# Attention into a gated FFN on one core: head 0's bias rows made in place, pads and V's ones set later on VectorE, a key row and a cast moved in front of V's loads

## The chip, the core and the metric

The kernel runs on one core of a Trainium2 chip. Its engines are TensorE (PE in the profile; its weight loads are PEld), VectorE (DVE), ScalarE (ACT), GpSimd (POOL) and SyncE (SP), each with its own instruction queue, and 16 DMA engines that all queues share. The metric is the device time of one execution in microseconds (us); the profile's times are those of one profiled execution.

## The reference

Eight batches of eight heads, 576 positions, head dimension 64. Selective attention: a causal softmax whose scores carry a bias from the running sum of the positive part of s. Its output, seen as 4608 tokens of 512, goes through a gated FFN of width 1536.

```python
def _attn_ref(q, k, v, s):
    scores = (1.0 / np.sqrt(D)) * np.matmul(q, k.transpose(0, 1, 3, 2))
    cum = np.cumsum(np.maximum(s, 0.0), axis=-1)
    bias = -(cum[:, :, :, None] - cum[:, :, None, :])
    scores = np.where(causal, -1000000000.0, scores + np.minimum(bias, 0.0))
    attn = softmax(scores)
    return np.matmul(attn, v)

def _moe_ref(x, w_gate, w_val, w_out):
    g = x @ w_gate
    return (g * sigmoid(g) * (x @ w_val)) @ w_out
```

All inputs and the output are float32.

## The kernel before

**Tiling.** Heads come in "head batches" of four (`hb`, 16 of them); head batch 0 is heads 0 to 3, head batch 1 heads 4 to 7. For each, k and q are loaded as float32 (`load_one`), cast to bf16 (`cast_half`, `cast_one`), transposed, and copied into `KQ[hb % 2][r]`. There are two such tiles per head batch, r = 0 for its first two heads and r = 1 for the others; in the text r is the row half. In the tile, 64 partitions hold the transposed k and q of those two heads, one beside the other (`e`), and the other 64 hold bias rows, of which four are used and the rest are zero. Thus one matmul of 128 partitions gives scores and bias together: the cumulated s is split into a high and a low bf16 part (`HL`), which stand in the query's or the key's rows against rows of constants near 1 and -1 (`ONES2`, `NEGS2`, each a 32-bit word holding two bf16). `aug` brings four bias rows of a head from `HL` into the tile by a DMA on SP's queue. `pads` zeroes 64 columns behind the keys, since the last key chunk of a head is 128 wide and reads 64 columns further.

**Scores and values.** `score_piece(bh, ci)` makes one of four pieces of a head's scores in a bank of PSUM (pieces 0 and 3 begin with a matmul of a mask, `lower`), and ScalarE's exponential (L369) takes it to `pt`. `av_piece` multiplies `pt` with `VT`, V in bf16 with a column of ones for the sum; `av_out` divides (L412, L413). `x_pe` transposes the attention output for the FFN. `init_vt` writes VT's ones and the zeros below its fifth chunk.

**The first stage.** The head batches 0 and 1 do not go through DRAM: TensorE transposes them against the identity (`pe_transpose_half`, L301; `pe_transpose`, L287) and `pe_out` copies from PSUM to `KQ` (L316 on VectorE, L314 on ScalarE). Of the eight banks, `take` gives the one that was given back longest ago, in program order. One bank (`spare`) serves `keep_warm`, matmuls of the identity whose result nobody reads; four hold the transposes of a head batch until the second row half is copied out.

**Order.** The program is under a manual schedule: each engine executes its instructions in the order written, and waits only for what an instruction needs. The order of the first stage is written out by hand. On VectorE: constants, the chain from s to `HL` (L226 to L232), copies of q for head batch 0, casts and copies of head batch 1, the cast of V's last chunk. On POOL: the mask, zeroes, the loads of head batch 1, `init_vt` and pads, a cast of q, V's loads (five DMAs), a weight load, casts of V. SP has s, the four loads of head batch 0, and then the `aug` DMAs, which follow from L232.

From head 8 on, a generator (`attn_items`) is pumped between the FFN's matmuls (L630, L687, L736).

## Time and profile before

| what | value |
|---|---|
| median of 5 runs | 375.87 us (375.82 to 377.81) |
| profiled execution | 375.86 us |
| its span | 374.1 us |
| mean granted TensorE clock | 1.000 |
| TensorE busy | 364.8 us (98%) |
| VectorE, ScalarE, POOL busy | 290.1, 240.7, 212.9 us |
| first exponential of scores | 11.36 us |
| first matmul of values | 19.54 us |

The span runs from the first to the last instruction; the execution's time has 1.8 us around it. Times in the profile count from the start of the span. A row of the timeline gives start, length, engine, line, operation, what it writes and reads with the shape, and how many; in brackets stand the idle time of the engine ahead of it and what ended it. A row of the waits gives the engine and line that waited, what for, the sum of the waits in us, their number, and the longest. Lines are those of the kernel before.

### The profile page before, as it was taken

What the parts mean: (1) busy time and instruction counts of PE and PEld (TensorE: products, weight loads), DVE (VectorE), ACT (ScalarE), POOL (GpSimd) and SP (SyncE); (2) the same over time, 40 slices, a digit from 0 to 9 for tenths busy, and PEclk for the clock granted to TensorE, in tenths of its full rate; (3) what the DMA queues carried; (4) which work ended last, traced back from release to release, by engine and by line L of the source; (5) the groups of instructions that cost most, each with busy time, mean ns of one, the idle gap of its engine ahead of it and who ended that gap; (6) DMA issues with size and microseconds to landing.
All of it is one profiled execution on the core that took longest, in us unless ns stands there. A gap on an engine that the chain in (4) does not pass through costs nothing.

```text
span 374.1 us, 8800 instructions
## 1 busy us (share of the span) xinstructions
PE 364.8 (98%) x3300; PEld 231.6 (62%) x3300; DVE 290.1 (78%) x578; ACT 240.7 (64%) x471; POOL 212.9 (57%) x325
## 2 busy tenths in 40 slices
PE   7899999999999999999999999999999999999995
PEld 6575556555555556855685559655865585476464
DVE  8968776468985999589967997699858867975984
ACT  8877776688876878588757875686566523323321
POOL 8982655856465647494649564955675516315320
PEclk9999999999999999999999999999999999999999
DMA  7799999799599997895879665995132103002003
GB/s 240 192 269 260 214 270 249 233 341 209 175 185 280 252 264 199 166 281 203 227 165 268 181 172 161 271 186 122 40 119 62 35 19 128 2 0 95 19 0 114
DMA packets 97147, 64.23 MB, mean 172 GB/s; under 512 B 77233, under 2 KB 82737, under 8 KB 97105
## 3 DMA queue, kind: packets, MB, share of 16 engines
q1 hardware_dynamic: 84976, 41.46, 46.8%
q0 software_dynamic: 12128, 22.21, 22.2%
q8 instruction: 26, 0.43, 0.5%
q14 instruction: 17, 0.13, 0.1%
HBM read 37.90 MB, written 19.86 MB: 154 GB/s over the span
## 4 chain that ended last, share of the span: by engine, by line
PE 90%; POOL 3%; ACT 2%; DVE 2%; issue 1%; DMA 1%; DVEq 0%; POOLq 0%; ACTq 0%
PE bank L630 47%; PE bank L736 17%; PE bank L359 11%; PE bank L396 8%; PE bank L687 6%; ACT pt L369 2%; DVE kq L316 1%; DMA kq<-HL 1%; PE bank L446 1%; DVE pp L653 1%; PE bank L287 1%; POOL vt L168 1%; DVE ht L664 1%; PE bank L353 1%; ACT kq L314 0%
## 5 line engine op out<-in xcount | busy, mean ns | idle before, releaser
L369 ACT ACTIVATE pt<-bank 128x512 bf16<-128x512 f32 (+1 forms) x256 | 120.3, 509 | 30.2 <-PE bank L359 17.0
L630 PE MATMUL bank<-XT,wg 128*128 128x512 bf16 x432 | 111.4, 379 | 0.5 <-DVE pp L653 0.3
L630 PE MATMUL bank<-XT,wv 128*128 128x512 bf16 x432 | 110.9, 379 | 0.1
L651 ACT ACTIVATE th<-bank 128x512 bf16<-128x512 f32 x108 | 64.7, 599 | 55.7 <-PE bank L630 52.2
L653 DVE SCALAR_TENSOR_TENSOR pp<-th,bank 128x512 bf16<-128x512 bf16 x108 | 73.6, 682 | 18.8 <-ACT th L651 18.3
L664 DVE SCALAR_TENSOR_TENSOR ht<-pp,bank 128x512 bf16<-128x512 bf16 x108 | 74.1, 686 | 10.6 <-PE bank L630 0.4
L359 PE MATMUL bank<-kq 128*128 128x128 bf16 (+4 forms) x576 | 75.8, 240 | 1.0 <-DMA kq<-HL 0.5
L673 POOL TENSOR_TENSOR ht<-ht 128x512 bf16<-128x512 bf16 x35 | 40.5, 1156 | 52.1 <-DVE su L671 52.0
L359 PEld LDWEIGHTS <-kq 128*128 128x128 bf16 x576 | 45.8, 98 | 31.4 <-issue 1.9
L630 PEld LDWEIGHTS <-wv 128*128 128x128 bf16 x432 | 38.4, 98 | 36.4 <-issue 0.6
L630 PEld LDWEIGHTS <-wg 128*128 128x128 bf16 x432 | 38.3, 98 | 34.2 <-issue 0.7
L374 POOL TENSOR_SCALAR_AFFINE_SELECT pt<-pt 128x512 bf16<-128x512 bf16 x56 | 36.9, 659 | 28.4 <-ACT pt L369 22.7
L396 PEld LDWEIGHTS <-pt 128*128 128x128 bf16 x960 | 41.7, 98 | 17.3
L396 PE MATMUL bank<-vt,pt 128*128 128x65 bf16 x960 | 46.9, 194 | 0.3 <-POOL vt L168 0.3
L430 POOL DMA_DIRECT2D xs<-ot x24 | 21.7, 906 | 29.9 <-DVE ot L413 27.6
L736 PEld LDWEIGHTS <-ht 128*128 128x128 bf16 x336 | 31.2, 98 | 4.3
L413 DVE TENSOR_TENSOR ot<-bank,rc 128x320 bf16<-128x320 f32 x64 | 31.4, 491 | 2.2
L183 POOL DMA_DIRECT2D kq<-HL x48 | 29.0, 606 | 0.0
L687 PE MATMUL bank<-wo,ht 128*128 128x512 bf16 x96 | 25.8, 379 | 0.0
L736 PEld LDWEIGHTS <-su 128*128 128x128 bf16 x252 | 23.6, 98 | 3.3
L801 POOL TENSOR_TENSOR ysb<-ysb 128x512 f32<-128x512 f32 x12 | 15.2, 1270 | 15.3 <-DVE ysb L795 15.3
L379 POOL TENSOR_SCALAR_AFFINE_SELECT pt<-pt 128x64 bf16<-128x64 bf16 x56 | 14.9, 267 | 15.6 <-ACT pt L369 15.5
(93 smaller groups left out, 388.0 us busy)
## 6 DMA issues: line engine op xcount, KB each, us to landing
out_dram<-ysb POOLq DMA_DIRECT2D x32, 256.0 KB, 4.5
rawv<-in_v_dram SPq DMA_DIRECT2D x28, 256.0 KB
rawk<-in_k_dram SPq DMA_DIRECT2D x12, 576.0 KB
rawq<-in_q_dram SPq DMA_DIRECT2D x12, 576.0 KB
xs<-ot POOLq DMA_DIRECT2D x24, 160.0 KB, 3.8
ks<-ck SPq DMA_DIRECT2D x11, 288.0 KB
qs<-cq SPq DMA_DIRECT2D x11, 288.0 KB
rawk<-in_k_dram POOLq DMA_DIRECT2D x3, 576.0 KB, 6.7
```

Of the source, the lines that this page charges most:

```text
L359: nc.tensor.matmul(sc[:, o : o + w], T[:, 1, e * S + 128 * tj : e * S + 128 * (tj + 1)], T[:, 0, e * S + lo : e * S + hi], start=not maske ...
L369: nc.scalar.activation(pt[:, c0 : c0 + n], sc, AF.Exp, scale=0.125)
L374: nc.gpsimd.affine_select(pt[:, 1088:1600], pt[:, 1088:1600], pattern=[[0, 4], [1, 128]], compare_op=ALU.is_ge, fill=zreg, base=0, channel ...
L396: nc.tensor.matmul(av[:, bi * (D + 1) : (bi + 1) * (D + 1)], pt[:, c0 : c0 + 128], VT[b % 2][:, tj, h, :], start=(tj == 0), stop=(tj == bi),)
L413: nc.vector.tensor_mul(ot[:, :, e * D : (e + 1) * D], av3[:, :, 0:D], rc[:, :, None].to_broadcast([128, NCH, D]),)
L630: nc.tensor.matmul(view(bs, TT), w[:, c, f0 : f0 + 128], xt[:, c, :], start=(c == 0), stop=(c == 3),)
L651: nc.scalar.activation(th, pg, AF.Tanh, scale=0.5)
L653: nc.vector.scalar_tensor_tensor(pp, in0=th, scalar=1.0, in1=pg, op0=ALU.add, op1=ALU.mult)
L664: nc.vector.scalar_tensor_tensor(hp[:, 2 * k2 : 2 * k2 + 2, :].rearrange("p a n -> p (a n)"), in0=pp, scalar=0.5, in1=pv, op0=ALU.mult, op ...
L673: (nc.vector if ft == NFT - 1 else nc.gpsimd).tensor_sub(hp[:, 1:3, :], hp[:, 1:4:2, :], hp[:, 0:3:2, :])
L687: nc.tensor.matmul(view(pys[ts_], DM), hps[ft // 2][:, 2 * (ft % 2) + half, c0 : c0 + 128], WO[j][:, ft % WKO, :], start=(ft == 0), stop=( ...
L736: nc.tensor.matmul(ps, lhs(p), rhs(p), start=(first and p == 0), stop=(last and p == NP - 1), skip_group_check=True,)
```

## The change

- `s_sb`, `c8` and `HL` get two more partitions (64 and 65). A second load, on ScalarE's queue, brings head 0's s into both.
- A column `less` is -1 everywhere but 0 in partition 64. The low part is now `less * high + c8`; so partition 64 holds the whole sum, rounded to bf16 (its high part) and partition 65 the low part, next to each other. The same instruction does both.
- Two engine copies put these two rows into head 0's key half (POOL, partitions 64 and 65) and query half (VectorE, partitions 96 and 97) of `KQ[0][0]`; the constants against them are two memsets on POOL. `aug` leaves head 0 out. Partitions 96 and 97 are zeroed on POOL before head batch 2 uses the tile.
- ScalarE zeroes one tile instead of two, POOL the other.
- On POOL the copy of the key row and the cast of q stand in front of V's loads with `init_vt(0)` and `pads(1)` gone from there; the memset of `aug_rows(1, 1)` goes behind V's loads. `pads(1)` and `init_vt(0)` move to VectorE, among and behind the copies of head batch 1.
- The second k copy of row half 1 goes from ScalarE to VectorE. The first three score pieces of head 0 stand between the k and q transposes of row half 1, and the fourth behind them; each of the two groups of ten keep-warm matmuls shrinks to four.
- The transposes of head batch 1 stand inside head 2 (behind its second and its fourth piece) instead of behind heads 0 and 1. The values of heads 0 and 1 go behind the scores of head 6.

```diff
--- before.py
+++ after.py
@@ -78,6 +78,7 @@
     )
 
     NPE = 5
+    LR = 66
     XB = 2
     KS = {i: dram.tile([NR * S, 128], BF16, name=f"ks{i}") for i in range(NPE, NHB)}
     XS = {
@@ -95,15 +96,16 @@
     VT = [const.tile([128, NCH, H, D + 1], BF16, name=f"vt{i}") for i in range(2)]
     ident = const.tile([128, 128], BF16)
     one_s = const.tile([128, 1], FP32)
-    HL = const.tile([BH, 4, 2, S], BF16)
+    HL = const.tile([LR, 4, 2, S], BF16)
     XR = 3 * TT
     XT = const.tile([128, 4, XR], BF16)
     warm = const.tile([128, 1], FP32)
     WS = const.tile([128, NFT // 2, 3, DM // 2], BF16)
     first_sbuf = ExitStack()
     first = first_sbuf.enter_context(tc.tile_pool(name="first", bufs=1))
-    s_sb = first.tile([BH, S], FP32)
-    c8 = first.tile([BH, S], FP32)
+    s_sb = first.tile([LR, S], FP32)
+    c8 = first.tile([LR, S], FP32)
+    less = first.tile([LR, 1], FP32)
     PTP = {0: first, "bufs": 7}
     lower = first.tile([128, 512], BF16)
 
@@ -180,15 +182,19 @@
                 r, e = divmod(hh, 2)
                 r0 = 64 * (1 - r)
                 bh = hb * HB + hh
+                if bh == 0:
+                    continue
                 engs[hh].dma_start(
                     KQ[hb % 2][r][r0 : r0 + 4, :, e * S : (e + 1) * S],
                     HL[bh : bh + 1, :, :, :],
                 )
 
-        nc.sync.dma_start(s_sb, s.rearrange("b h n -> (b h) n"))
-        def init_vt(i):
-            nc.gpsimd.memset(VT[i][:, :, :, D : D + 1], 1.0)
-            nc.gpsimd.memset(VT[i][64:128, 4, :, 0:D], 0.0)
+        nc.sync.dma_start(s_sb[0:BH, :], s.rearrange("b h n -> (b h) n"))
+        nc.scalar.dma_start(s_sb[BH:LR, :], s[0, 0:1, :].to_broadcast([LR - BH, S]))
+
+        def init_vt(i, eng=nc.gpsimd):
+            eng.memset(VT[i][:, :, :, D : D + 1], 1.0)
+            eng.memset(VT[i][64:128, 4, :, 0:D], 0.0)
 
         for r in range(NR):
             load_one(0, "k", (r, r + 1))
@@ -197,8 +203,10 @@
         nc.vector.memset(warm, 0.0)
         nc.vector.memset(one_s, 1.0)
         nc.scalar.activation(warm, warm, AF.Exp)
-        nc.vector.memset(HL[:, 0:2, 0, :].bitcast(FP32), ONES2)
-        nc.vector.memset(HL[:, 2:4, 1, :].bitcast(FP32), NEGS2)
+        nc.vector.memset(HL[0:BH, 0:2, 0, :].bitcast(FP32), ONES2)
+        nc.vector.memset(HL[0:BH, 2:4, 1, :].bitcast(FP32), NEGS2)
+        nc.vector.memset(less, -1.0)
+        nc.vector.memset(less[BH : BH + 1, :], 0.0)
         make_identity(nc, ident)
         nc.gpsimd.memset(lower, 0.0)
         nc.gpsimd.affine_select(
@@ -206,30 +214,36 @@
             compare_op=ALU.is_ge, fill=nc.gpsimd.to_reg(MASKED), base=0, channel_multiplier=-1,
         )
 
-        def pads(i):
+        def pads(i, eng=nc.gpsimd):
             for r in range(2):
-                nc.gpsimd.memset(KQ[i][r][64 * r : 64 * r + 64, :, NR * S :], 0.0)
+                eng.memset(KQ[i][r][64 * r : 64 * r + 64, :, NR * S :], 0.0)
 
         for r in range(2):
             nc.gpsimd.memset(aug_rows(0, r)[:, 1, :], 0.0)
-            nc.scalar.mul(
-                KQ[0][r][64 * (1 - r) : 64 * (1 - r) + 64, 0, :],
-                one_s[0:64, 0:1].to_broadcast([64, NR * S + 64]), 0.0,
-            )
+            if r == 0:
+                nc.scalar.mul(
+                    KQ[0][0][64:128, 0, :], one_s[0:64, 0:1].to_broadcast([64, NR * S + 64]), 0.0
+                )
+                nc.gpsimd.memset(KQ[0][0][96:98, 1, 0:S].bitcast(FP32), NEGS2)
         pads(0)
+        nc.gpsimd.memset(KQ[0][0][64:66, 0, 0:S].bitcast(FP32), ONES2)
+        nc.gpsimd.memset(aug_rows(0, 1)[:, 0, :], 0.0)
         nc.vector.memset(aug_rows(1, 0), 0.0)
         for nm in ("k", "q"):
             load_one(1, nm, eng=nc.gpsimd)
-        init_vt(0)
-        pads(1)
 
         nc.vector.tensor_scalar(s_sb, s_sb, 0.0, 8.0, ALU.max, ALU.mult)
         nc.vector.tensor_tensor_scan(
-            c8, one_s[0:BH, 0:1].to_broadcast([BH, S]), s_sb, 0.0, ALU.mult, ALU.add
+            c8, one_s[0:LR, 0:1].to_broadcast([LR, S]), s_sb, 0.0, ALU.mult, ALU.add
         )
         nc.vector.tensor_copy(HL[:, 0, 1, :], c8)
-        nc.vector.tensor_sub(HL[:, 1, 1, :], c8, HL[:, 0, 1, :])
-        nc.vector.tensor_copy(HL[:, 2:4, 0, :], HL[:, 0:2, 1, :])
+        nc.vector.scalar_tensor_tensor(
+            HL[:, 1, 1, :], in0=HL[:, 0, 1, :], scalar=less, in1=c8,
+            op0=ALU.mult, op1=ALU.add,
+        )
+        nc.gpsimd.tensor_copy(KQ[0][0][64:66, 1, 0:S], HL[BH:LR, 1, 1, :])
+        nc.vector.tensor_copy(KQ[0][0][96:98, 0, 0:S], HL[BH:LR, 1, 1, :])
+        nc.vector.tensor_copy(HL[0:BH, 2:4, 0, :], HL[0:BH, 0:2, 1, :])
 
         SP4 = [nc.sync] * 4
         GP4 = [nc.gpsimd] * 4
@@ -883,11 +897,11 @@
             for _ in range(n):
                 nc.tensor.matmul(view(spare, 128), ident, ident, start=True, stop=True)
 
-        def row_half(nm, r, eng):
+        def row_half(nm, r, eng, eng1=None):
             for g in range(2):
                 pe_transpose_half(0, nm, g, r)
             for g in range(2):
-                pe_out(0, nm, g, r, eng)
+                pe_out(0, nm, g, r, (eng, eng1 or eng)[g])
 
         def half_batch(nm):
             for g in range(2):
@@ -911,14 +925,17 @@
         row_half("q", 0, nc.vector)
         cast_half(0, "k", 1, nc.scalar)
         cast_half(0, "q", 1, nc.gpsimd)
+        load_v(0, range(5), nc.gpsimd)
         nc.gpsimd.memset(aug_rows(1, 1), 0.0)
-        load_v(0, range(5), nc.gpsimd)
         w_load("g", 0)
         aug(1, SP4)
-        keep_warm(10)
-        row_half("k", 1, nc.scalar)
+        keep_warm(4)
+        row_half("k", 1, nc.scalar, nc.vector)
+        for ci in range(3):
+            score_piece(0, ci)
         row_half("q", 1, nc.vector)
-        keep_warm(10)
+        keep_warm(4)
+        score_piece(0, 3)
         cast_one(1, "k", nc.vector)
         cast_one(1, "q", nc.vector)
         for c in range(3):
@@ -931,16 +948,21 @@
         for nm in ("g", "v"):
             w_load(nm, 1, 0)
         load_one(3, "k", eng=nc.gpsimd)
-        scores(0)
+        scores(1)
+        for ci in (0, 1):
+            score_piece(2, ci)
         half_batch("k")
-        scores(1)
+        for ci in (2, 3):
+            score_piece(2, ci)
         half_batch("q")
-        scores(2)
         scores(3)
+        pads(1, nc.vector)
         for nm in ("k", "q"):
             for g in range(2):
                 pe_out(1, nm, g, 1, nc.vector)
+        init_vt(0, nc.vector)
         cast_v(0, 4, nc.vector)
+        nc.gpsimd.memset(KQ[0][0][96:98, 0, 0:S].bitcast(FP32), 0.0)
         aug(2, SP4)
         cast_one(2, "k", nc.gpsimd)
         cast_one(2, "q", nc.gpsimd)
@@ -950,8 +972,8 @@
         init_vt(1)
         scores(4)
         scores(5)
+        scores(6)
         values(0, 1)
-        scores(6)
         values(2, 3)
         scores(7)
         aug(3, SP4)
```

## The prediction

> **What bounds the kernel now.** I read the page first. TensorE is busy for 98% of the span, and the chain that ended last lies on it for 90%: what the change can touch is how early that chain begins, the first 25 us.
>
> ```profile
> span 374.1 us, 8800 instructions
> PE 364.8 (98%) x3300; PEld 231.6 (62%) x3300; DVE 290.1 (78%) x578; ACT 240.7 (64%) x471; POOL 212.9 (57%) x325
> PE 90%; POOL 3%; ACT 2%; DVE 2%; issue 1%; DMA 1%; DVEq 0%; POOLq 0%; ACTq 0%
> ```
>
> Second, the waits of 8 to 16 us: TensorE waits for the bias rows' DMA, and ScalarE, which has the exponentials, for TensorE's first scores.
>
> ```profile
> ACT pt L369 <- PE bank L359: 1.3, 1, 1.3
> PEld L359 <- DMA kq<-HL: 0.9, 1, 0.9
> ```
>
> Third, the timelines of ScalarE, VectorE and TensorE over 0 to 32 us (start, length, engine, line, what).
>
> ```profile
> 8.71 1.37 ACT L314 COPY kq<-bank 64x640 bf16<-64x640 bf16 x2 [0.56 <-PE bank L301]
> 11.36 13.52 ACT L369 ACTIVATE pt<-bank 128x512 bf16<-128x512 f32 x32 [1.28 <-PE bank L359]
> ```
>
> ```profile
> 7.18 0.53 DVE L232 COPY HL<-HL 64x1152 bf16<-64x1152 bf16 x1
> 7.63 1.43 DVE L316 COPY kq<-bank 64x640 bf16<-64x640 bf16 x2
> 9.21 1.46 DVE L316 COPY kq<-bank 64x640 bf16<-64x640 bf16 x2
> 10.70 0.76 DVE L246 CAST ck<-rawk 128x1152 bf16<-128x1152 f32 x1
> 11.38 1.12 DVE L246 CAST cq<-rawq 128x1152 bf16<-128x1152 f32 x1
> 12.53 5.64 DVE L316 COPY kq<-bank 64x640 bf16<-64x640 bf16 x8
> 18.92 0.42 DVE L168 CAST vt<-rawv 64x512 bf16<-64x512 f32 x1 [0.75 <-DMA rawv<-in_v_dram]
> ```
>
> ```profile
> 10.93 0.83 PE L359 MATMUL bank<-kq 128*128 128x128 bf16 x8 [0.55 <-DMA kq<-HL]
> 18.61 0.38 PE L353 MATMUL bank<-lower,ident 128*128 128x512 bf16 x1
> 19.54 1.08 PE L396 MATMUL bank<-vt,pt 128*128 128x65 bf16 x30
> 20.46 0.38 PE L353 MATMUL bank<-lower,ident 128*128 128x512 bf16 x1
> 22.50 0.38 PE L353 MATMUL bank<-lower,ident 128*128 128x512 bf16 x1
> 23.43 0.52 PE L446 MATMUL bank<-ident,ot 128*128 128x128 bf16 x5
> 23.88 1.08 PE L396 MATMUL bank<-vt,pt 128*128 128x65 bf16 x30
> ```
>
> ScalarE runs its 32 exponentials without a break from 11.36 to 24.88. VectorE is full from 3.79 to 18.17, where the last of the eight copies of batch 1 (heads 4 to 7) ends. Head 6, the first to need the last copies, begins on TensorE only at 20.46, so VectorE has 20.46-18.17 = 2.3 us to spare. TensorE has no gap to speak of from 17.62 on.
>
> **The change, part by part.** *Bias rows of head 0.* The DMA that began at 7.80 and landed at 10.88 (3.08 us in the chain) is gone for head 0; two small engine copies take its place. Head 0 then waits for the copies of q (row half 0) on VectorE. That is earlier, but not by the whole of 3.08, and the fourth score piece of head 0 still waits for head 1's DMA: its 128 key columns reach 64 columns into head 1.
>
> VectorE up to there, with the engine's durations: the scalar_tensor_tensor in place of the subtraction has the same 576 elements from two sources, so 0.75 again, ending 7.14. Two more partitions cost nothing. The two `less` memsets (0.06 each, row L197) fit into the idle 0.29 before L220. The key copy of 2x576 is half of L232's elements: 0.53/2 and the gap of 0.04, 0.3 to 0.35. (Bounds: 0.2, and 0.53.) L232 so ends at 8.05, q's two copies (1.43) at 9.46 against 9.06. First scores at 9.5, and the first exponential 0.43 later as before (10.93 to 11.36), at 9.95 instead of 11.36: **1.4 us earlier**. On ScalarE this fits: it gives the second k copy (0.72) away and is free at 9.46.
>
> The second s load, on ScalarE's queue, holds ScalarE for about what SP's took (0.59); the one zeroing removed (1.21) more than covers it, and the k cast at 4.76 waits for the load (landed 4.74) anyway. It should land by s_sb's 3.77, which only delays things if it is later.
>
> *VectorE behind it.* The k copy taken from ScalarE (64x512, 0.71) comes next: 9.49 to 10.2. Then q of row half 1; but its TensorE transposes now stand behind three score pieces of head 0. Eight score matmuls took 0.67 from first start to next start (10.93 to 11.60), so these transposes start at 10.2, and in before VectorE started 0.48 after the first of them (8.73 to 9.21): 10.65, an idle 0.45. Two copies (1.46) to 12.1; the casts of batch 1 (0.76 and 1.12, overlapping to 1.8) to 13.95; four copies of 5.64/8 each to 16.8; the pads, now here, two memsets of 64 elements, 0.13 each with their gap by the rows of L197 and L200, 0.26; four more copies, **19.9 against 18.17**. The transposes of batch 1, now inside head 2, are in time: TensorE reaches them at about 12.95 and 14.6, VectorE wants their results at 13.95 and 15.4. The four terms: key copy 0.35, k copy 0.73, transposes behind the scores 0.4, pads 0.26, 1.74 in all. Then V's ones and zeros (0.1 and 0.5) and its cast (0.42), to about 21.0 against 19.34.
>
> *TensorE then.* Two banks that the last q copies free are head 5's, and head 6 reads what they write, so TensorE passes 19.9 with these left, by the starts in the rows above: the end of head 5 (0.27), head 6 (18.61 to 19.54, 0.93), the values of heads 0 and 1 (19.54 to 20.46, 0.92) which now stand behind head 6, those of 2 and 3 (0.91), head 7 (22.50 to 23.43, 0.93), the transposes of x (0.45). 19.9+0.27+0.93+0.92+0.91+0.93+0.45 = 24.35. In before the values of heads 4 and 5 start at 23.88. So: **+0.45 us**. V's last cast, 21.0, meets the first values at 21.1: just covered; if it were later by x, all is. Moving the values behind head 6 is what makes the late ones and zeros bearable; without it they would hold head 6.
>
> ScalarE's exponentials of head 7 then run from 23.6 to 25.2, and the values of heads 6 and 7 want them at 25.7: not the bound. The early start is spent in ScalarE waiting around 17 us (head 4 needs q of batch 1, 16.8) and 19 to 20 us.
>
> *POOL.* Off its queue ahead of batch 1's k and q loads: nothing; added there: two memsets of 2x288 (half of L214's 0.60, 0.3 each) and one of 0.60 that was ScalarE's. The loads issue 1.3 to 1.4 later, so they land at 11.0 and 12.4 at worst, against 9.62 and 11.04; VectorE wants them at 12.1 and 12.85. Covered by 0.4, at worst. The key copy on POOL (nearest row, the cast of 128x576: 0.66) ends near 8.1, before 9.5. Removed behind the loads: V's ones and zeros (0.97) and the pads (0.65); the memset of 1.10 goes behind V's loads, which so issue about 0.8 earlier. The first weight load and V's casts stay where they were within 0.4, and V is wanted only at 21. The zeroing of the key rows (0.3) lies in POOL's idle time before the batch 2 cast (0.78, waiting for a load). SP has one bias DMA less, and the others go out 0.4 to 0.5 earlier than before.
>
> *Keep-warm.* Twelve matmuls fewer. Rows: the nine transposes of k from 5.49 take 1.14, the nine of q from 6.45 take 0.68, so the clock rose there; it never falls later though TensorE idles up to 0.55 between bursts (10.38 to 10.93). The Trainium skill (TensorE: Matmul & The Clock Gate, Part 4) says transposes do not count as activity, and Part 1 that one idle window of about 3.4 us halves the clock. Counting only real matmuls, the new gap is from the four at 7.1 to head 0 at 9.5, about 2.2 us: below that window, so row and rule give nothing. Were it to fall, for one window from about 9.9: 0.67 for the score pieces and 0.28 for five transposes double, so q's copies come up to 0.9 later, and all behind them. I take zero and keep 0.9 for the range.
>
> A second rule speaks against the order on POOL: the skill's SBUF — State Buffer (section SBUF: two separate sides) says that VectorE copies with two ports and POOL's descriptor writing shut each other out. The rows agree in part: V's issues took 0.70 to 1.47 and one cast 1.12 where the other took 0.76. In the new order V's issues (8.8 to 13.8) still lie beside both casts, so I keep the sum of 1.88. By the rule both could take 1.12: +0.36.
>
> From 24 us on the order is untouched, and the chain is TensorE, VectorE and ScalarE work that follows; the weight and batch 2 loads landed 2 us before use. I carry +0.45 to the end: 375.86 for the profiled execution (374.1 span and 1.8 around it; the median is 375.87, the same) gives **376.3**.
>
> **The rivals.** (1) *VectorE decides, a small loss or nothing*: 376.3, within about 0.7 either way (375.6 to 377.0) by the bounds of key copy, pads, wait for transposes, and arrival of s. Chance 0.70. For it: the 1.74 against the 2.3 that were spare, less the 0.92 of values that used to lie inside that spare time.
> (2) *The early start survives*: if VectorE keeps enough slack (its copies shorter, or the banks in another rhythm), the 1.4 us of the first exponential pass on: 374.5. For it: ScalarE's unbroken 13.52. Against: head 4 cannot start before 16.8. Chance 0.07; a part of it falls under (1).
> (3) *Slower, batch 1's q load late*: its issue goes from 5.33 to 6.7, behind three more instructions, with V's loads now closer behind and the lock above. It decides from a landing of 12.85 on, one for one; at 13.7 all is 0.85 later, 377.2. For it: issue to landing was 5.7. Against: the DMA share fell to 0.74 in 8 to 11 us, so a later load finds room. With the clock case, which has the same size, chance 0.23; a third of it ends under the bound.
> (4) *The change does not do what it says* (head 0 still waits for a DMA): only for its fourth piece, as said; part of (1).
>
> **How the numbers follow.** About 0.3%, 1.1 us, is what a measurement of this kernel can tell from no change: below 374.7 or above 377.0. Faster: (2) and a little, 0.08. Slower: two thirds of (3) and the upper end of (1), 0.20. Same: 0.72. The range, 375.0 to 377.6, leaves out most of (2) and the far end of (3).
>
> **What would show it.** Right: first exponential near 10.0; VectorE's eight copies of batch 1 ending near 19.9, with an idle gap near 10.3; ScalarE waiting near 17 us; values of heads 0 and 1 after head 6, near 21.1; values of heads 4 and 5 at 24.3. Wrong: VectorE done by 19.0 or earlier; a wait of the batch 1 casts on their loads; matmul pitch doubled anywhere after 6.5; or an end that moved by more than that 24.3 says, which would put the cause behind 25 us.

## The result, and the profile after

| | kernel before | changed kernel |
|---|---|---|
| median | 376.80 us (77 runs, 375.78 to 378.81) | 378.29 us (40 runs, 376.93 to 380.92) |
| ratio | 1 | 1.0043, 95% interval 1.0035 to 1.0052 |
| profiled execution, its span | 375.86, 374.1 us | 377.64, 375.7 us |
| first exponential | 11.36 us | 10.38 us |
| last copy of head batch 1 on VectorE ends | 18.17 us | 20.16 us |
| values of heads 4 and 5 start | 23.88 us | 25.26 us |

The change makes the kernel slower by 0.43%, some 1.6 us (the two medians differ by 1.49, 0.40%). The forecast was +0.45 us on the profiled execution, 0.12%: the right sign, far too small. Its absolute number, 376.3, lay low for a second reason: the median of the first five runs, 375.87, is low among the 77 runs of the same kernel, whose median is 376.8. What follows counts in differences and ratios. Each ratio is against runs of the kernel before that were taken beside it, and medians from different occasions are not compared. One experiment, e13, was profiled only in a disturbed execution, and so has times alone.

Where the loss arises: from the start of values 4 and 5 to the end of the span there are 350.2 us in the kernel before and 350.4 in the changed one, so 1.4 of the 1.6 us by which the span grew lie ahead of that, in the first stage. In the undisturbed profiles of the other kernels that rest takes 350.2 to 351.5 us (353.0 in e12), whatever the first stage did; so a single profile says little on the whole time to less than 1 us, and what follows reads the stage.

The page of the changed kernel. TensorE is still busy for nearly all of the span, and the chain that ended last now has more of POOL and of DMA in it (5% and 2%, against 3% and 1%):

```profile
span 375.7 us, 8793 instructions
PE 365.3 (97%) x3288; PEld 231.2 (62%) x3288; DVE 292.5 (78%) x586; ACT 239.0 (64%) x469; POOL 214.1 (57%) x326
PE 88%; POOL 5%; DVE 2%; DMA 2%; ACT 1%; issue 1%; SPq 0%; DVEq 0%; POOLq 0%; ACTq 0%
```

ScalarE's timeline of the changed kernel (start, length, engine, line, what; in brackets the idle time ahead and what ended it). In the kernel before this was one unbroken row of 32 exponentials from 11.36 to 24.88. Now it begins 1.0 us earlier and is broken three times; the pause of 1.64 ahead of head 7 alone is more than the early start:

```profile
10.38 1.84 ACT L383 ACTIVATE pt<-bank 128x512 bf16<-128x512 f32 x4 [0.92 <-PE bank L373]
12.43 6.85 ACT L383 ACTIVATE pt<-bank 128x512 bf16<-128x512 f32 x16 [0.22 <-PE bank L373]
19.50 3.43 ACT L383 ACTIVATE pt<-bank 128x512 bf16<-128x512 f32 x8 [0.22 <-PE bank L373]
24.57 1.69 ACT L383 ACTIVATE pt<-bank 128x512 bf16<-128x512 f32 x4 [1.64 <-PE bank L373]
```

VectorE's timeline. L246 is the old L232, L330 the old L316, L260 the old L246, L219 the pads, L196 and L197 V's ones and zeros:

```profile
3.83 0.75 DVE L235 TENSOR_SCALAR s_sb<-s_sb 66x576 f32<-66x576 f32 x1 [0.23 <-DMA s_sb<-in_s_dram]
7.41 0.30 DVE L245 COPY kq<-HL 2x576 bf16<-2x576 bf16 x1
7.75 0.80 DVE L246 COPY HL<-HL 64x1152 bf16<-64x1152 bf16 x1
8.47 2.19 DVE L330 COPY kq<-bank 64x640 bf16<-64x640 bf16 x3
11.21 1.47 DVE L330 COPY kq<-bank 64x640 bf16<-64x640 bf16 x2 [0.55 <-PE bank L315]
12.71 0.76 DVE L260 CAST ck<-rawk 128x1152 bf16<-128x1152 f32 x1
13.39 0.91 DVE L260 CAST cq<-rawq 128x1152 bf16<-128x1152 f32 x1
17.35 2.81 DVE L330 COPY kq<-bank 64x640 bf16<-64x640 bf16 x4
21.14 0.42 DVE L170 CAST vt<-rawv 64x512 bf16<-64x512 f32 x1
```

The reader is to see where the 1.99 us between 18.17 and 20.16 come from: the row chain, L235 to L246, ends at 8.55 where it ended at 7.70 (+0.85); the third copy of 2.19 is the k copy that ScalarE had (+0.73); then 0.55 of waiting for q's transposes, for 0.15 in the kernel before. The pads add 0.2 net, and the casts take 0.2 less.

TensorE's timeline at the end of the stage. Head 5 waits twice for VectorE's last copies; head 6's fourth piece, whose key columns reach into head 7, waits for the DMA of head 7's bias rows; and the 60 matmuls of values stand ahead of head 7:

```profile
18.86 0.38 PE L367 MATMUL bank<-lower,ident 128*128 128x512 bf16 x1 [0.41 <-DVE kq L330]
20.21 0.38 PE L373 MATMUL bank<-kq 128*128 128x320 bf16 x2 [0.25 <-DVE kq L330]
20.49 0.38 PE L367 MATMUL bank<-lower,ident 128*128 128x512 bf16 x1
21.95 0.20 PE L373 MATMUL bank<-kq 128*128 128x64 bf16 x1 [0.39 <-DMA kq<-HL]
22.05 1.99 PE L410 MATMUL bank<-vt,pt 128*128 128x65 bf16 x60
25.26 1.08 PE L410 MATMUL bank<-vt,pt 128*128 128x65 bf16 x30
```

That DMA is late because of an edit of which I had counted only the gain. The chain of waits of the changed kernel, in order of time (start, length, what):

```profile
9.07 4.67 POOL rawv L159 x5
13.74 1.61 POOL kq L929
15.35 0.02 issue
15.37 0.61 SPq L187
15.98 0.04 issue
16.03 5.88 DMA kq<-HL
21.90 0.05 issue
```

L929 is the zeroing that the change put behind V's loads. SP's bias DMAs of heads 6 and 7 write into the tile that it zeroes: they go out at 15.37 and 16.03, where the kernel before had issued its last two at 12.11 and 12.78.

### The profile page after: what moved, and what is told of

Read it like the earlier page. It is cut to its first block, busy times and chain, and to the rows that moved or that the text cites. A ratio compares the mean times of both kernels' runs of the same rounds, so it can differ in the third digit from the quotient of the medians.

```text
span 375.7 us, 8793 instructions
## 1 busy us (share of the span) xinstructions
PE 365.3 (97%) x3288; PEld 231.2 (62%) x3288; DVE 292.5 (78%) x586; ACT 239.0 (64%) x469; POOL 214.1 (57%) x326
## 4 chain that ended last, share of the span: by engine, by line
PE 88%; POOL 5%; DVE 2%; DMA 2%; ACT 1%; issue 1%; SPq 0%; DVEq 0%; POOLq 0%; ACTq 0%
PE bank L644 47%; PE bank L750 17%; PE bank L373 10%; PE bank L410 8%; PE bank L701 6%; DMA kq<-HL 2%; POOL rawv L159 1%; DVE kq L330 1%; PE bank L460 1%; DVE pp L667 1%; POOL vt L170 1%; DVE ht L678 1%; ACT pt L383 1%; PE bank L301 1%; POOL kq L929 0%
## 5 line engine op out<-in xcount | busy, mean ns | idle before, releaser
L750 PEld LDWEIGHTS <-su 128*128 128x128 bf16 x252 | 23.6, 98 | 3.3
```

The lines of the kernel that those rows point to most:

```text
L750: nc.tensor.matmul(ps, lhs(p), rhs(p), start=(first and p == 0), stop=(last and p == NP - 1), skip_group_check=True,)
```

## The experiments

Seventeen kernels are new and one, r1_after, repeats the changed kernel. All ratios are against runs of the kernel before taken beside the kernel. "Last copy" is the end of VectorE's copies of head batch 1, "values 4,5" the start of those values on TensorE; both are from one profiled execution each, the ratio from 7 to 40 executions.

| kernel | ratio (95% interval) | last copy | values 4,5 |
|---|---|---|---|
| before | 1 | 18.17 | 23.88 |
| changed | 1.0043 (1.0035 to 1.0052) | 20.16 | 25.26 |
| r1_after, the same again | 1.0026 (1.0005 to 1.0047) | 20.22 | 24.69 |
| e1_memset_early | 1.0026 (1.0001 to 1.0052) | 20.37 | 24.85 |
| e2_q_first | 1.0019 (1.0004 to 1.0033) | 20.47 | 24.95 |
| e3_both | 1.0026 (1.0007 to 1.0045) | 20.50 | 25.02 |
| e4_before_memset_late | 0.9999 (0.9981 to 1.0016) | | 26.69 |
| e5_pool_pads | 1.0012 (0.9996 to 1.0028) | 20.72 | 25.20 |
| e6_old_order | 1.0019 (1.0007 to 1.0031) | 20.22 | 25.81 |
| e7_rows_only | 1.0015 (1.0002 to 1.0029) | 19.15 | 24.59 |
| e8_rows_first | 1.0051 (1.0036 to 1.0066) | 20.08 | 25.52 |
| e9_rows_values6 | 1.0015 (1.0002 to 1.0028) | 19.14 | 24.93 |
| e10_rows_dve | 1.0065 (1.0044 to 1.0085) | 19.27 | 25.02 |
| e11_after_warm10 | 1.0020 (1.0009 to 1.0032) | 21.34 | 25.81 |
| e12_pieces | 1.0033 (1.0016 to 1.0050) | 19.14 | 24.94 |
| e13_early_warm10 | 1.0012 (0.9997 to 1.0027) | | |
| e14_before_warm4 | 1.0002 (0.9986 to 1.0018) | 18.69 | 24.34 |
| e15_k_scalar | 1.0041 (1.0024 to 1.0057) | 22.94 | 28.54 |
| e16_before_collide | 1.0011 (0.9999 to 1.0024) | 19.03 | 24.96 |
| e17_after_memset_mid | 1.0033 (1.0016 to 1.0051) | 20.37 | 24.84 |

No version beats the kernel before. e5, e7, e9 and e13 lie at 1.0012 to 1.0015, below the changed kernel. The intervals are wide: most versions can be told from the kernel before or from the changed one, and few from each other.

### The zeroing behind V's loads: e1, e4, e17

e1 moves it back in the changed kernel, e17 half way, e4 moves it back in the kernel before:

```diff
 e1:   +nc.gpsimd.memset(aug_rows(1, 1), 0.0)
        load_v(0, range(5), nc.gpsimd)
       -nc.gpsimd.memset(aug_rows(1, 1), 0.0)
 e17:  +load_v(0, range(2), nc.gpsimd)
        nc.gpsimd.memset(aug_rows(1, 1), 0.0)
       +load_v(0, range(2, 5), nc.gpsimd)
 e4:   the same two lines of before, swapped
```

> The changed kernel with the zeroing of aug_rows(1, 1) back in front of V's loads on GpSimd; all else as changed. Theory A (two chains end within half a microsecond of each other: the bias DMAs of heads 6 and 7, which wait for this zeroing and landed at 21.90, and VectorE's work up to V's last cast, 21.56): the DMA wait of TensorE at 21.95 goes, the values begin near 21.6 instead of 22.05, and the end is 0.4 us earlier than in the changed kernel, that is 1.2 us over the kernel before, ratio 1.003. Theory B (the late zeroing is the whole loss): back at the kernel before, ratio 1.000. Theory C (the bias DMAs are late because V's loads now fill the DMA engines, wherever the zeroing stands): still a wait near 21.9, ratio 1.0043.

> The kernel before with one edit: the zeroing of aug_rows(1, 1) behind V's loads on GpSimd. The bias DMAs of heads 6 and 7 then go out near 14.7 and 15.3 instead of 12.1 and 12.8. Theory A: they land between 19.5 and 21.5, and head 6's fourth piece comes on TensorE at 21.5, so it costs nothing to 0.3 us, ratio 1.000 to 1.001. Theory B: it costs what the whole change costs, ratio 1.004.

> The changed kernel with the zeroing of L929 behind V's second load in place of the fifth: 10.8 to 11.9, beside VectorE's copies from PSUM and not beside its casts (12.7 to 14.5), and in time for SP's bias DMAs of heads 6 and 7. Theory L with A: no cast over 1.15, no wait of TensorE for the bias rows of head 6, hardly a run over 378.7 (the changed kernel had 17 of 40, r1_after 6 of 20), values 4 and 5 near 24.85, ratio 1.0015 to 1.0028. Theory C2 (V's loads are early enough to crowd the other transfers, and make the long runs): three of V's loads move by 1.1, the long runs stay, 1.003 to 1.0045.

In e1 and in e17 TensorE no longer waits for these bias rows; values 4 and 5 start at 24.85 and 24.84, 0.4 before the changed kernel's profile and still 0.97 behind the kernel before. 0.97 us of 376.8 are 0.26%, and e1 measured 1.0026; with an interval of 1.0001 to 1.0052 that close agreement is in part luck. e17 measured 1.0033 (1.0016 to 1.0051), more than the 1.0015 to 1.0028 that its theory gave and inside what rival C2, V's loads crowding the other transfers, had named; against C2 stands one run of ten over 378.7, and nothing else was tried on it. So there is a part without the late zeroing: theory B, that it is all, falls by e17's interval. That the late zeroing costs something is seen in the profile (TensorE's wait), and not shown by the ratios, whose intervals overlap. In the kernel before the same swap costs nothing that can be measured (e4; its profiled execution was one of its longest, with head 0's scores held up to 12.56 by the landing of the bias rows and TensorE at half clock from 13.90 to 17.31 behind that wait, so its row of the table is not read). The repeat of the changed kernel adds a warning:

> The changed kernel again, as it is, beside the other three. All theories: 1.0043 within 0.0015, and a second profile: values 4 and 5 near 25.2; exponentials earlier by 1 us than in the kernel before and stalled for 1.5 to 2 us in front of head 7's.

TensorE's timeline of r1_after. The zeroing stood at the same place and the DMAs of heads 6 and 7 landed in time: the values follow head 6 without a wait, and those of heads 4 and 5 come at 24.69, 0.57 earlier than in the first profile of the same program. Neither the 25.2 nor the 1.0043 within 0.0015 that I expected came back, and 1.0026 is e1's ratio too:

```profile
21.48 1.99 PE L410 MATMUL bank<-vt,pt 128*128 128x65 bf16 x60
24.69 1.08 PE L410 MATMUL bank<-vt,pt 128*128 128x65 bf16 x30
```

So that wait of TensorE for the bias rows is there in one of two profiles, not in every execution.

### The terms on VectorE: e2, e3, e15, e5

e2 puts q's transposes of row half 1 in front of head 0's pieces, which should take away VectorE's wait of 0.55; e3 is e1 and e2 together; e15 gives the k copy back to ScalarE; e5 is e1 with pads and V's ones on POOL, behind V's loads.

```diff
 e2:    row_half("k", 1, nc.scalar, nc.vector)
       +for g in range(2):
       +    pe_transpose_half(0, "q", g, 1)
        for ci in range(3):
            score_piece(0, ci)
       -row_half("q", 1, nc.vector)
       +for g in range(2):
       +    pe_out(0, "q", g, 1, nc.vector)
 e15:  -row_half("k", 1, nc.scalar, nc.vector)
       +row_half("k", 1, nc.scalar)
 e5:    load_v(0, range(5), nc.gpsimd)
       +pads(1)
       +init_vt(0)
       -pads(1, nc.vector)
       -init_vt(0, nc.vector)
```

> The changed kernel with the transposes of q (row half 1) in front of the three score pieces of head 0 instead of behind them; all else as changed. VectorE's idle 0.55 us at 11.2 should go and its chain end 0.55 us earlier (V's last cast at 21.0). Theory A: TensorE still waits for head 7's bias rows until about 21.9, so the end moves by 0.1 us at most, ratio 1.004. If VectorE's chain alone decides: 0.55 us earlier, 1.05 us over the kernel before, ratio 1.0028. Theory B: no change, ratio 1.0043.

> Both edits: the zeroing of aug_rows(1, 1) in front of V's loads, and the transposes of q in front of head 0's score pieces. Theory A: more than the sum of the two alone, since each uncovers the other: values begin near 21.0 instead of 22.05, the end 1.0 us earlier than in the changed kernel, 0.6 us over the kernel before, ratio 1.0016. Theory B: ratio 1.000, as with the zeroing alone. Theory C: as with the zeroing alone, ratio 1.004.

> The changed kernel with the second k copy of row half 1 on ScalarE again, where before had it (VectorE loses a 128x512-element copy of 0.73). The sum of the prediction counts it at 0.73 on VectorE's chain: copies of batch 1 end 0.7 earlier, 19.5 in place of 20.16, ratio 0.001 to 0.0015 under r1_after's. Theory W (it was taken up by the wait of 0.55 behind it, in which VectorE waits for q's transposes, which TensorE has behind head 0's three pieces): q's copies begin at 11.2 as before it, copies end within 0.2 of 20.16, the same ratio as r1_after within 0.0007.

> The changed kernel with the zeroing of L929 back in front of V's loads (as in e1_memset_early) and with batch 1's pads and V's ones and zeros set on POOL again, behind V's loads, not on VectorE. Theory A (VectorE's instructions up to V's last cast decide when the values start): VectorE gives up two pads of 0.28 in front of batch 1's copies of row half 1 and two settings of 0.09 and 0.48 with 0.2 to 0.4 of gaps in front of V's cast. In e1 the copies ended at 20.37 and V's cast at 21.78; they should end at about 19.8 and 20.5, values 0 and 1 should start near 21.0 in place of 21.63, and the ratio should be 1.0010 to 1.0015 where e1 had 1.0026. Rival D (TensorE's own sum of work up to the values decides, V's cast has room): values stay within 0.2 us of 21.63 and the ratio at 1.0026. Rival P (POOL's casts of V, which now stand 1.9 us later, take the place): the values wait for POOL and the ratio is 1.003 or more.

None did what a sum of terms says. In e2 VectorE's wait of 0.55 left its place, and one of 0.67 for batch 1's transposes of k came instead: last copy 20.47, no earlier than in e1. In e3 that wait is 0.81. e15 gave VectorE 0.73 less to do and was not faster than r1_after, which ran beside it (1.0041 and 1.0026, overlapping intervals): in its profile the wait behind that copy is 2.08, which holds the 0.73, the 0.55 and 0.8 of the half clock told of below. That profile is of e15's longest execution (380.9), so its row of the table is no typical one. e5's ratio fits what was expected (1.0012), but its interval holds no change and e1's ratio too, and its profile had the half clock as well, so it shows no mechanism.

One sum did hold: from the end of the last copy to values 4 and 5 there are 4.47 to 4.48 us in r1_after, e1, e2 and e17 (24.69-20.22, 24.85-20.37, 24.95-20.47, 24.84-20.37). The prediction had 4.45 for this.

### The rows alone: e6 to e10, e12

e6 is e1 with the order of the kernel before on TensorE, both keep-warms of 10 and the k copy on ScalarE; e7 is e6 with pads and ones on POOL behind V's loads and with the values in front of head 6, so that of the change only the rows in place remain; e8 is e7 with pads and ones in their old place in front of the casts; e9 is e7 with the values behind head 6; e10 is e9 with both row copies on VectorE (the one that moves is the key half's); e12 is e9 with three pieces of head 0 early, q's transposes in front of them and the second keep-warm at 4.

```diff
 e6 against e1:
       -keep_warm(4)
       -row_half("k", 1, nc.scalar, nc.vector)
       -for ci in range(3):
       -    score_piece(0, ci)
       +keep_warm(10)
       +row_half("k", 1, nc.scalar)
        row_half("q", 1, nc.vector)
       -keep_warm(4)
       -score_piece(0, 3)
       +keep_warm(10)
 ...
       -scores(1)
       -for ci in (0, 1):
       -    score_piece(2, ci)
       +scores(0)
        half_batch("k")
       -for ci in (2, 3):
       -    score_piece(2, ci)
       +scores(1)
        half_batch("q")
       +scores(2)
        scores(3)
 e10 against e9:
       -nc.gpsimd.tensor_copy(KQ[0][0][64:66, 1, 0:S], HL[BH:LR, 1, 1, :])
       +nc.vector.tensor_copy(KQ[0][0][64:66, 1, 0:S], HL[BH:LR, 1, 1, :])
```

> The changed kernel with the zeroing of L929 in front of V's loads, and with the order on TensorE as it was (head 0's scores whole and behind row half 1 of q, both keep-warms of 10, batch 1's half batches behind head 0 and head 1, the second k copy on ScalarE); rows of head 0 in place, pads and ones late on VectorE, and the values behind head 6 stay. Theory A (VectorE decides): VectorE gives up the k copy of 0.73 and the 0.55 of waiting behind head 0's pieces, so batch 1's copies end near 19.2 in place of 20.37, V's cast near 20.6, values 0 and 1 start near 20.7, and the ratio is about 1.000. Rival D (TensorE's sum, in which the values stand behind head 6): TensorE is not shorter with 12 more keep-warm matmuls, values at 21.6 and the ratio 1.0026. Rival O (the place of the values behind head 6 is what costs): also 1.002 or more, but with V's cast early and TensorE busy with head 6's scores when V is ready.

> e6_old_order with the values in front of head 6 again and batch 1's pads and V's ones on POOL behind V's loads: of the change only head 0's rows in place, its row cast order on POOL and V's earlier loads are left. Theory A: VectorE has the old chain plus the key copy of 0.30 and the slower subtraction; batch 1's copies end near 18.9, V's cast near 19.5, values at 19.6 to 20.0; first exponential near 10.4 where before had 11.36, of which little arrives; ratio 0.998 to 1.0005. Rival D (the rows in place themselves cost, by the two engines' shared work around the cumulative sum): 1.001 to 1.003. Rival P (POOL's casts of V late): values wait for POOL, 1.002.

> As e7_rows_only, but with pads and V's ones and zeros on POOL in their old place in front of POOL's casts of batch 0, so that only head 0's rows in place are left of the change (their POOL instructions stand in front of V's loads, which issue later). Theory A: POOL's row instructions and the old 1.9 us in front of the casts put the q cast and V's loads later than in e7 by about 1.9 us; the first exponential goes to about 11.5 and the values to 20 or later; ratio 1.000 to 1.002. Rival D (the pads' place is indifferent, rows alone decide): the same ratio as e7_rows_only within 0.0010.

e7 is the clearest of them: the in-place rows, with pads and ones behind V's loads, cost 0.15% (1.0002 to 1.0029). ScalarE's timeline of e7, and TensorE's row that explains its break:

```profile
11.47 1.69 ACT L383 ACTIVATE pt<-bank 128x512 bf16<-128x512 f32 x4 [1.56 <-PE bank L373]
13.65 11.94 ACT L383 ACTIVATE pt<-bank 128x512 bf16<-128x512 f32 x28 [0.48 <-PE bank L373]
```

```profile
12.50 0.68 PE L301 MATMUL bank<-ident,ck 128*128 128x128 bf16 x9 [0.22 <-DVE ck L260]
```

The first exponential is no earlier than in the kernel before (11.36), since here head 0 stands behind row half 1 and the keep-warm. VectorE's row chain ends 0.84 later (8.54 for 7.70), so its k cast of batch 1 comes at 11.43 for 10.70 and, at 1.01 for 0.76, ends 0.98 later; the transposes of k wait for it, head 1's scores stand behind them, and ScalarE restarts at 13.65. From there its stream is unbroken and ends at 25.58, 0.70 behind the kernel before. Measured: 0.57 us.

e8 is far worse than expected. POOL's timeline has the row copy and the cast of q (L246 and L272 by this kernel's own line numbers) behind pads and ones, and TensorE waits for that cast:

```profile
9.18 0.66 POOL L246 COPY kq<-HL 2x576 bf16<-2x576 bf16 x1
9.90 0.66 POOL L272 CAST cq<-rawq 128x576 bf16<-128x576 f32 x1
```

```profile
10.61 0.69 PE L317 MATMUL bank<-ident,cq 128*64 128x128 bf16 x9 [1.97 <-POOL cq L272]
```

So moving pads and ones out of POOL's way was needed once the rows were made there: from e7 to e8 it is 0.36%.

e6 came to 1.0019, not to the 1.000 of theory A. Its profile cannot say why: TensorE's matmuls of 128 columns took 0.31 us up to 10.3 us (0.22 from 6.4 on in the kernel before), which put q's copies at 10.73 for 9.93 in e7.

> e7_rows_only with the values of heads 0 and 1 behind head 6's scores, as in the changed kernel. Theory A (two bounds on the start of values 4 and 5: the last VectorE copy of batch 1 plus 4.48 us, which the profiles of e1, e2, e3 and e5 share within 0.05, and V's last cast plus what stands behind it): copies end near 19.15 as in e7 and V's last cast (POOL) near 20.06, head 6's scores fill TensorE until then, values 4 and 5 start at 23.6 to 23.8 where e7 had 24.59 and before 23.88; ratio 0.9990 to 1.0005. Rival O (the place of the values behind head 6 costs by itself): 1.002 or more. Rival T (TensorE's sum is the same in either order): as e7, 1.0015.

> e9_rows_values6 with the copy of head 0's query row (2x576, 0.71 on POOL) on VectorE too, in front of the key row's copy. Theory A with sharing (a bf16 or f32 copy of VectorE from SBUF to SBUF stands still while POOL has a tensor instruction running: L246 takes 0.80 beside POOL's 0.71 where L232 took 0.53, and ends 0.31 after it): VectorE pays 0.30 more and gets 0.2 to 0.3 back in L246, its chain ends within 0.1 of e9's, POOL's cast of q ends at about 8.4 in place of 9.06, the q transposes and V's loads come 0.6 earlier; ratio 0.0005 to 0.001 under e9's. Rival S (no sharing; L246 is slow for another reason): VectorE's chain ends 0.30 later, ratio 0.0008 above e9's.

> e9_rows_values6 with three pieces of head 0's scores in front of the second keep-warm, which has 4, with q's transposes of row half 1 in front of them: the early start of the exponentials without the k copy, pads and ones on VectorE. Theory A: first exponential near 10.7 in place of 11.5, but VectorE's copies of batch 1 end near 19.1 as in e9 and the values start as there: the same ratio as e9 within 0.0007. Rival X (the exponentials' stream on ScalarE decides, so that an earlier first one arrives at the end): 0.0015 to 0.002 under e9's.

e9 against e7 prices the place of the values where VectorE is not late: values 4 and 5 at 24.93 for 24.59, with a pause of 0.42 ahead of head 7's exponentials that e7 hasn't; the ratios are equal (1.0015), so no more than that profile is shown. I had expected 23.6: TensorE waits there for the exponentials (0.20 and 0.27 up to head 4, 0.28 ahead of the values), not for the copies, and the 4.48 does not apply. e12 has its first exponential at 10.92, e9 at 11.48, and values 4 and 5 come at 24.94 and 24.93: in these two an early first exponential arrives nowhere, and e12's ratio, 1.0033, is not under e9's as rival X had it. Why it is above was not seen; the profiled execution is e12's longest (379.72), and what is long in it lies behind 25 us. e10 was expected to gain and measured 1.0065, with runs from 377.4 to 381.7; the one profile was of a short run, with values 4 and 5 at 25.02. What makes its long runs was not seen.

### Two instructions that shut each other out: e11, e15, e16

> The changed kernel with both keep_warm calls at 10 matmuls, as they were, and nothing else altered. Rival C (TensorE's clock: with 4 in place of 10 it is idle for longer between 7 and 10 us, and in the profiles of e3 and e5 the granted clock fell to 0.5 to 0.6 there, which puts q's copies and all behind them up to 0.8 later): in those executions in which the clock falls the loss goes, so the median comes down, to about 1.002 to 1.003, and the runs lie closer together. Theory A without the clock: 12 matmuls of 0.07 us each on TensorE are hidden, or cost up to 0.8 us in front of head 0's pieces; 1.0043 to 1.006.

e11 restores `keep_warm(10)` twice in the changed kernel. Its profile had something else in it. VectorE's timeline, then POOL's:

```profile
12.70 0.76 DVE L260 CAST ck<-rawk 128x1152 bf16<-128x1152 f32 x1
13.38 2.09 DVE L260 CAST cq<-rawq 128x1152 bf16<-128x1152 f32 x1
```

```profile
13.72 1.13 POOL L929 MEMSET kq<- 64x1216 f32 x1
14.78 0.99 POOL L346 DMA_DIRECT2D wg<-in_moe_w_gate_dram  x1
```

In the changed kernel's own profiles the same two instructions start at the same times, and the cast takes 0.91 and the zeroing 1.61. In each of these profiles one of the two pays: 0.91 and 1.61, or 2.09 and 1.13. Where it is the cast, the last copy ends at 21.34 and values 4 and 5 start at 25.81. e15 has both casts caught, one by the zeroing and one by the casts of V; VectorE's timeline and POOL's:

```profile
13.48 1.50 DVE L260 CAST ck<-rawk 128x1152 bf16<-128x1152 f32 x1
14.90 2.17 DVE L260 CAST cq<-rawq 128x1152 bf16<-128x1152 f32 x1
```

```profile
13.23 1.13 POOL L929 MEMSET kq<- 64x1216 f32 x1
14.29 0.99 POOL L346 DMA_DIRECT2D wg<-in_moe_w_gate_dram  x1
15.28 1.17 POOL L170 CAST vt<-rawv 128x512 bf16<-128x512 f32 x2
```

The cast of k ends at 14.98, 0.62 behind the zeroing (14.36), the cast of q at 17.07, 0.62 behind V's second cast (16.45): the cast ends the same 0.62 behind POOL's instruction in all three (15.47 and 14.85 in e11), as if it stood while that ran. The collision takes two edits: the zeroing moved to 13.7, and VectorE's added work, which moved the casts from between 10.7 and 12.5 to between 12.7 and 14.3. In e4, with the zeroing late and VectorE as before, the casts end at 13.03 and the zeroing starts at 13.30: they miss each other, and no cost of the swap could be measured.

> The kernel before with POOL's zeroing of L914 moved from in front of V's loads to behind the first of them, to 10.5 from 8.5, so that it runs beside VectorE's k cast of batch 1 (10.7). Theory L (a tensor instruction of POOL and a cast of VectorE from SBUF to SBUF exclude each other): one of them is stretched; where it is the cast, it takes 1.1 to 1.9 where it took 0.76, batch 1's transposes and head 1's scores behind them are later by up to 1.1, ScalarE stalls there, ratio 1.001 to 1.003; where it is the zeroing, it takes 1.6 to 1.9 in place of 1.1, V's other loads are 0.5 later, 1.000. Without L (the order of SP, V's loads or VectorE's instructions decide): both keep their times and the ratio is 0.9995 to 1.0005.

e16 was to make the collision in the kernel before. It did not come about: `load_v(0, range(1), nc.gpsimd)` in front of the zeroing put it at 9.38 to 10.51, and the k cast began at 10.58. V's next two loads took 1.38 and 1.39 beside the casts, and in the profile the bias rows of head 0 landed 1.1 late, at 12.0. Its 1.0011 (0.9999 to 1.0024) says nothing on the collision.

### The keep-warm matmuls: e11, e13, e14

e13 is e1 with `keep_warm(10)` twice, e14 the kernel before with `keep_warm(4)` twice.

> The changed kernel with both keep_warm calls at 10 and with the zeroing of L929 in front of V's loads; VectorE's additions, the order and the values behind head 6 are left. Theory A with C (the three parts add up: clock 0.8, zeroing 0.4 to 0.6, VectorE the rest): 1.0005 to 1.0015, and values 4 and 5 at 24.4 to 24.9. Theory A without C: as e1, 1.0026, values 4 and 5 near 24.85. Rival D (the parts don't add, each undone alone takes what can be had): 1.0020, as e11.

> The kernel before with both keep_warm calls at 4 in place of 10, nothing else. Theory C: the granted clock falls in some executions between 8 and 12 us (matmuls of 0.31 us where they take 0.22), q's transposes or head 0's scores are late by up to 1 us, ratio 1.001 to 1.003 with a wider spread of runs. Without C: head 0's scores wait for the bias rows' landing anyway (10.9), so 0.9995 to 1.0005.

e14: nothing to be measured in the kernel before, where head 0's scores wait for the bias rows anyway. In the changed kernel it is different. The stretches of e15 (TensorE's granted clock is the number behind POOL's busy time and count):

```profile
6.00:8.00 2.00, 1.02 (x13) 0.75 (x13) 1.83 (x4) 2.00 (x4) 1.95 (x3) 1.00 0.49 129
8.00:10.00 2.00, 1.71 (x11) 1.06 (x12) 1.90 (x3) 1.21 (x3) 1.93 (x4) 0.57 0.87 359
10.00:12.00 2.00, 2.00 (x17) 1.37 (x16) 0.02 (x1) 1.69 (x4) 2.00 (x3) 0.58 0.93 294
```

In e15 and e5 the matmuls of 128 columns take 0.31 from 8.2 to 11.6, 0.22 on both sides; in e3 from 8.9 to 12.3. So of the eight profiles with four keep-warm matmuls and the new order three have a stretch of about 3.4 us at half clock around the transposes of q, and q's copies start at 11.98 in e15 and 11.97 in e5, for 11.21 in the profiles that have this order and not the stretch. Less of it is left at the end of the stage: values 4 and 5 come 0.35 later in e5 than in e1, though e5 has the pads (0.28) off VectorE, and 0.07 later in e3 than in e2. No profile with ten keep-warm matmuls (e13's aside) had the clock fall again between 8 and 12 us, e11 among them, though in e6 it came up late and in e4 it fell at 13.90.

Which profiles have it goes with how much TensorE had to do in the stretch of 3.41 us before, counted from where the clock had first risen. TensorE was busy for 1.78 us of it in e3 (5.46 to 8.87), 1.95 in e15 and 1.97 in e5 (both from about 4.85), and the clock fell; for 2.01 in e2 (6.50 to 9.91), 2.04 in e17, 2.22 to 2.43 in r1_after, the changed kernel and e1, and it stayed. These kernels give TensorE nearly the same work there; what differs most is where the stretch begins, 4.84 to 7.47. No sharp limit follows: in e15 the clock fell once more, from 21.92 to 25.33, behind 2.09, and in e16 it stayed behind 1.98. The Trainium skill (TensorE: Matmul & The Clock Gate, Part 1) says that a window of about 3.4 us, which runs freely, decides on the clock, and that its phase differs from run to run: the length and the phases agree. In none of the stretches that led to a fall was TensorE idle throughout, as the page's "idle window" would have it.

The ratios with the keep-warm restored are lower: e11's 1.0020 and e13's 1.0012 lie clear of the changed kernel's first 1.0043, but overlap with r1_after's 1.0026, which is the same kernel again and ran beside e13. e13 came out as expected with the clock counted in (1.0005 to 1.0015), but its interval holds what was expected without it too. That the keep-warm is worth something in the changed kernel is likely from the profiles and not shown by the times.

### What is settled and what is not

Shown: in the profiles of r1_after, e1 and e17, which have none of the events named next, the stage ends 0.81 to 0.97 us late, by VectorE's longer chain; the ratios of the three, 1.0026, 1.0026 and 1.0033, agree with that, within wide intervals (1.0001 to 1.0052). Shown as well: three events that add to it in some executions only, the wait for the bias rows (0.6), a stretched cast (1.1 and more), and the half clock (0.8 at q's copies in e5 and e15, 0.1 to 0.4 at the end of the stage in e3 and e5; the second one in e15 some 1.1 by itself, 28.54-22.94 for the 4.48 elsewhere). Runs of over 378.7 us agree with this without proving it: 17 of 40 of the changed kernel, 6 of 20 and 9 of 20 in r1_after and e15; with the zeroing out of the way none of 7 and of 8 in e1 and e3, 2 of 22 in e5, 1 of 10 in e17, and with the ten keep-warms 1 of 22 in e11; the kernel before has 1 of 77, and beside the other kernels from none of 30 to 3 of 36. But e2, which has the late zeroing and the fewer keep-warms, has none of 10, and e10 and e8, which have neither, 15 of 22 and 10 of 16 (e12, with one of the two keep-warms at 4, has 4 of 16). What each of the three events has in the remaining 0.65 us or so of the measured ratio (1.62 less 0.97) stays open; so do the long runs of e10.

## Why the prediction was wrong

**The mechanism held.** Rival (1), that VectorE's batch 1 decides and the early exponential is spent in waiting, is what happened in the profiles of r1_after, e1 and e17; in the first profile of the changed kernel the DMA of head 7's bias rows ended later still. ScalarE's long wait was not near 17 us or at 19 to 20 us, where it was expected, but ahead of head 7 (1.64). The first exponential came 1.0 us earlier (1.4 was expected, and the row chain below has the difference), and nothing of it arrived; an idle gap on VectorE ahead of q's copies measured 0.55 where 0.45 was expected; the k copy 0.73 as said; the pads 0.28 for 0.26. From the last copy to values 4 and 5 the prediction took 4.45 (its six terms add up to 4.41, so to 24.31 and not 24.35) and the runs showed 4.48. The loads of batch 1 landed at 10.18 and 12.44 and were not waited for: rival (3) did not happen, nor did rival (2).

**The term that was mis-sized: the row chain.** The same durations as before and a key copy of 0.30 to 0.35 put the end of the old L232 at 8.05. It ended at 8.55. The two more partitions did cost nothing (the scan took 1.35 in both), and the copy of two rows on VectorE was right (0.30). But L235 took 0.75 where L226 took 0.54, and the copy L246 0.80 where L232 took 0.53: 0.48 together, and the other differences cancel to 0.02. Each of the two had a POOL instruction beside it that the change had moved or put there:

```profile
3.67 0.60 POOL L222 MEMSET kq<- 64x608 f32 x1
7.52 0.71 POOL L244 COPY kq<-HL 2x576 bf16<-2x576 bf16 x1
```

The profiles show that this is what stretches them: L235 ends at 4.57 to 4.58 whether it starts at 3.63 (e7) or at 3.99 (e2), 0.31 behind that zeroing, which ends at 4.26, and L246 ends 0.31 behind POOL's row copy (8.54 and 8.23). In e10, where POOL has no row copy, its cast of q ends at 8.56 and L246 at 8.87: 0.31 again. With 8.55 for 8.05 the prediction's own sum gives +0.95 in place of +0.45 (+0.93 with its terms added up rightly), and e1 and e17 show +0.97.

**The choice behind it.** I set the rule of the Trainium skill (SBUF — State Buffer, section SBUF: two separate sides), by which VectorE's two-port instructions and POOL's shut each other out, against the rows of before, and kept the rows. But the rows of before were no durations of the engine alone: L226 and L232 had been held by POOL's pads already. The first of the two pads ahead of L232 is in the chain of the kernel before:

```profile
3.79 0.54 DVE L226 TENSOR_SCALAR s_sb<-s_sb 64x576 f32<-64x576 f32 x1 [0.22 <-DMA s_sb<-in_s_dram]
7.19 0.20 POOL kq L211
```

That pad ends at 7.39, and L232 (7.18 and 0.53) at 7.70, 0.31 behind; L226 ends at 4.33, 0.31 behind the end of a pad at 4.02. In e4, e14 and e16 POOL stands a little otherwise, and the two end 0.31 behind other POOL instructions. So all twenty profiles agree with the rule in that VectorE's instruction stands while POOL's runs, and none shows either of the two by itself. Their lengths are a wait and a rest of 0.31, and such a length can't be carried over to an order in which POOL does something else beside it. By the rule the places to go through were every VectorE copy or cast from SBUF to SBUF beside every POOL instruction of the new order; I went through V's loads only, and counted 0.36 at most.

**The step that was missing: who waits for the moved zeroing.** "The memset of 1.10 goes behind V's loads, which so issue about 0.8 earlier" counted what the move does for POOL. It did not ask who waits for the zeroing. SP's DMAs for heads 6 and 7 do, and they went from 12.11 and 12.78 to 15.37 and 16.03; "The others go out 0.4 to 0.5 earlier than before" was wrong for all: the DMA of head 1 went out at 8.65 for 8.67, since L246, which they all wait for, ended 0.85 later. And the zeroing came to lie beside the casts of batch 1, which the same change had moved by 2 us.

**The keep-warm.** "I take zero and keep 0.9" had the size at q's copies right (0.8 in e5 and e15), and the zero wrong for a part of the executions. The step that failed is "below that window, so row and rule give nothing", which asks only for a gap as long as the window: the clock fell behind 3.41 us of which TensorE had worked 1.78 to 1.97, with no gap over 0.9. Whether the transposes count as activity these profiles do not say. One profile of the changed kernel would not have shown the fall; it takes several.

## What to carry to other kernels

When an instruction is moved back on its queue, list who reads or overwrites what it writes, on every queue, DMA queues first, and what it will then run beside. Before a duration of a VectorE copy between SBUF tiles is carried over, see what POOL did beside it: here a length of 0.53 held a wait of 0.2 for POOL, and became 0.80 when POOL's instruction beside it changed. Where a change puts work on POOL there, add POOL's remaining time, not nothing. And where a change touches several queues, edits that cost nothing one by one can meet: for the late zeroing and for the fewer keep-warms no cost could be measured in the kernel before (0.9999 and 1.0002).

## What the hardware showed that I had not expected

- The same two instructions with the same starts, a cast of 128x1152 on VectorE at 13.38 and a zeroing of 64x1216 on POOL at 13.72, came out both ways: cast 0.91 and zeroing 1.61 in two profiles, cast 2.09 and zeroing 1.13 in a third. The Trainium skill (SBUF — State Buffer, SBUF: two separate sides) has it that the one that starts first holds the shared port for the whole instruction; in e11 the cast had started 0.34 earlier and lost. POOL was still issuing a load of V when the cast began (12.55 to 13.73), which may be why; no run here separates that.
- VectorE's copies out of PSUM kept their times beside the same zeroing (0.82 in e4, 0.83 in e17, where 0.80 to 0.83 is what the same copy takes elsewhere). Those that were stretched go from SBUF to SBUF.
- Landings vary between profiles by as much as the effects under study: head 0's scores, which wait for its bias rows, began at 10.93 in the profile of the kernel before, at 11.37 in e14, which leaves all DMAs alone, and at 12.00 in e16 and 12.56 in e4. These two do not move that DMA, but issue V's first load 1.1 us earlier (8.47 and 8.46 for 9.57); how much of it that load has was not separated.
